# Chunk 1 of x loaded plainly and turned by TensorE, and the second linear layer's queries of chunk 0 computed inside attention 1

## The chip, the cores and the metric

The kernel runs on one core of one Trainium2 chip. The metric is the device time of one execution in microseconds (us), from runs without the profiler; the kernel before takes 2224.86 us (median of three runs, 2223.25 to 2225.45). A core has TensorE (PE, which loads weights beside its matmuls: PEld), VectorE (DVE), ScalarE (ACT), GpSimd (POOL) and SyncE (SP), each with an instruction stream of its own that it works through in order. Transfers are issued from the queues of SP, ACT and POOL and carried by 16 DMA engines.

## The reference

Two layer kinds alternate, A, B, A, B, each added to x (2048 tokens, 1024 features, bf16; 32 heads of 32). The second A and B use the same weights as the first.

```python
def _A_ref(x, wqkv, w_phi, wo):          # linear attention
    q, k, v = qkv[0], qkv[1], qkv[2]     # x @ wqkv, split into heads
    pq = jnp.einsum("bhsd,hdf->bhsf", q, w_phi)
    pk = jnp.einsum("bhsd,hdf->bhsf", k, w_phi)
    phi_q = jnp.concatenate([_softmax(pq, axis=-1), _softmax(-pq, axis=-1)], axis=-1)
    phi_k = jnp.concatenate([_softmax(pk, axis=-1), _softmax(-pk, axis=-1)], axis=-1)
    kv = jnp.einsum("bhsf,bhsd->bhfd", phi_k, v)
    z  = jnp.einsum("bhsf->bhf", phi_k)
    num = jnp.einsum("bhqf,bhfd->bhqd", phi_q, kv)
    den = jnp.einsum("bhqf,bhf->bhq", phi_q, z)[..., None] + 1e-6
    return (num / den) ... @ wo
def _B_ref(x, wqkv, wo):                 # softmax attention
    scores = jnp.einsum("bhqd,bhkd->bhqk", q, k) * (Dh ** -0.5)
    o = jnp.einsum("bhqk,bhkd->bhqd", _softmax(scores, axis=-1), v)
    return o ... @ wo
x = x + _A_ref(_layernorm(x), ...)
x = x + _B_ref(_layernorm(x), ...)
x = x + _A_ref(_layernorm(x), ...)
x = x + _B_ref(_layernorm(x), ...)
```

## The kernel before

x is held in SBUF as xT, features on the partitions, in four chunks of 512 tokens. The four layers run one behind the other as linear stage 1, attention 1, linear stage 2, attention 2, and each pair overlaps at its seam. The weight w_phi is folded into the key and query weights once, in linear stage 1 (fold_phi); the folded weights go to two tensors in HBM, wd_k and wd_q, and are read back as slabs.

Nothing in the code gives the order of the instructions directly. Every operation is recorded with an engine, an estimated duration, its dependencies, its buffers and a priority; then a planner (Sched) plays the engines through and emits each engine's stream in the order in which its model starts them. The tables of numbers at the head of the file are priorities, quotas of buffers and due times for it, so a change to them moves instructions in the whole program. Where the planner finds PE idle in an attention, it inserts filler matmuls: one kind reads xT and onesD (line 616, shared with the layer norms' means), the other xT and zero (line 1788). A unit of PE work is four matmuls of 32 output rows side by side, each 512 columns wide, with the line of mm (L616).

Start. load_x brings chunk 0 of x half by transposing loads on SP (L653) and half by plain loads on POOL that PE turns against the identity (L665); chunks 1, and 2 with 3, come by transposing loads on SP. fold_phi brings the key weight wnat as two quarters on ACT's queue (L825) and one half on POOL's (L828), PE turns it in eight groups (L841), ACT and DVE copy each group out of PSUM (L849, L846), PE folds phi in (L616, reading phi_t), and ACT and DVE copy the folded slab out (L875, L878); SP stores it (L884). The value weights come as slabs on SP (L798). The layer norm of a chunk squares x (L722, L727), sums on PE (L689), and normalizes on DVE (L770, L773 or L778, L782). a_keys then makes a chunk's keys and values for each token tile, their exponentials (L984), the sums (L988) and the products (L945), and kv_sum the state (L911).

Attention 1. A step is up to three score matmuls (L1468), one exponential on ACT that reads them (L1484, 1536 or 1024 wide) and later the products with the values and ones (L1516). Some halves of a step are taken off ACT: exp_dve computes a pair of them by a polynomial on DVE (L1366 twice, then L1375, L1378, L1380, L1383, L1385); COUNT says how many in each turn. Between the steps PE gets the rest as filling work through one PSUM bank, number 7: the keys, values and queries of later turns, the output products of finished chunks, and linear stage 2's layer norms, keys and values of chunks 0, 1 and 2. Results leave bank 7 over DVE (L1216 among others). The normalized chunks 0, 1 and 2 are written to xd in HBM (L1776) and read back in linear stage 2 (L1655).

Linear stage 2. Attention 1's last outputs, the layer norm, keys and values of chunk 3, and the rest of chunk 2's (L1021 to L1036); then for each chunk in two halves the queries: four groups of eight units against wd_q, two exponentials for each group (L1108), their totals (L1119), two logarithms (L1125, L1127), a difference (L1129), its exponential (L1132), a spread over the heads (L1088), the products (L1136, L1151, L1159, L1166, L1171, L1174, L1177); then a_out and the layer norm before attention 2.

## Time and profile before

| | |
|---|---|
| median of 3 runs | 2224.86 us |
| profiled execution | 2226.66 us, span 2224.9 us |
| PE, DVE, ACT, POOL busy in the span | 2153.5, 1803.5, 1968.9, 204.4 us |
| granted TensorE clock | 1.00 of full speed throughout |
| matmuls | 37014 |
| DMA | 111.08 MB, mean 50 GB/s |

A row of the groups reads: line, engine, operation, output<-input, shape and count | busy us, mean ns of one | idle time of the engine before them and who ended it. A row of the windows reads: from:to, length, then for each engine its busy us and, in brackets, its instructions, then the granted clock, the mean busy share of the DMA engines and GB/s. A row of the timeline reads: start, length, engine, line, operation. Busy time of a group is not its count times its mean where matmuls overlap.

### The profile page before, as it was taken

To read this page: it belongs to the slowest core of one execution; us is meant where nothing else is said; L and a number is where in the kernel's file an instruction comes from. 1 tells how busy PE (TensorE), PEld (TensorE's weight loads), DVE (VectorE), ACT (ScalarE), POOL (GpSimd) and SP (SyncE) were. 2 spreads that over 40 slices of the span, in tenths; PEclk is the share of its full clock that TensorE was granted. 3 is DMA by queue.
4 is the path that set the end of the run, shared out by engine and by line. 5 is a ranking of instruction groups with operands and counts; after the bars stand their busy time and mean duration, and the time that the engine had idled before them with its cause. 6 is when DMAs were issued, how large, how long until landed. Compare 5 with 4: busy or idle time off the path is not lost. (4 is left out here: it accounts for less than half of the span.)

```text
span 2224.9 us, 83188 instructions
## 1 busy us (share of the span) xinstructions
PE 2153.5 (97%) x37014; PEld 864.4 (39%) x37014; DVE 1803.5 (81%) x2839; ACT 1968.9 (88%) x1913; POOL 204.4 (9%) x303
## 2 busy tenths in 40 slices
PE   6999999999999999999999999999999999999999
PEld 4554454344333333333333544434333433223333
DVE  6886553597898988785586864599999999999998
ACT  3536668999999999999998667899999999999998
POOL 1010010000002011201224200000000000100000
PEclk9999999999999999999999999999999999999999
DMA  9320111110113122212335101110010011200101
GB/s 201 73 59 10 29 32 32 45 26 19 38 48 109 42 69 73 75 44 73 102 97 154 42 5 32 31 34 22 24 43 21 19 26 29 58 24 28 45 26 38
DMA packets 122256, 111.08 MB, mean 50 GB/s; under 512 B 57960, under 2 KB 107944, under 8 KB 121896
## 3 DMA queue, kind: packets, MB, share of 16 engines
q0 software_dynamic: 17744, 57.23, 9.2%
q1 hardware_dynamic: 101496, 46.96, 8.9%
q8 instruction: 289, 4.73, 0.9%
q10 hardware_dynamic: 2656, 1.57, 0.3%
q14 instruction: 71, 0.58, 0.1%
HBM read 71.11 MB, written 13.89 MB: 38 GB/s over the span
## 5 line engine op out<-in xcount | busy, mean ns | idle before, releaser
L1484 ACT ACTIVATE arena<-psum 128x1536 bf16<-128x1536 f32 (+1 forms) x1339 | 1615.5, 1379 | 21.2 <-PE psum L1516 7.3
L616 PE MATMUL psum<-arena 128*32 128x512 bf16 (+2 forms) x18944 | 1068.9, 352 | 13.0 <-DMA arena<-in_B_wo_dram 3.7
L616 PEld LDWEIGHTS <-arena 128*32 128x32 bf16 x19456 | 462.5, 96 | 441.7 <-issue 177.6
L1516 PE MATMUL psum<-arena 128*32 128x512 bf16 x4096 | 618.8, 383 | 6.2 <-DVE arena L1532 5.9
L1516 PE MATMUL psum<-arena,ones_bf 128*32 128x512 bf16 x4096 | 619.0, 383 | 0.0
L1468 PE MATMUL psum<-arena 32*128 32x512 bf16 x4016 | 528.4, 384 | 18.9 <-ACT arena L1484 14.1
L1468 PEld LDWEIGHTS <-arena 32*128 32x128 bf16 x4016 | 149.0, 91 | 530.7 <-issue 523.7
L1366 DVE TENSOR_SCALAR arena<-psum 128x512 int32<-128x512 f32 x462 | 311.4, 681 | 51.8 <-PE psum L1468 45.8
L1385 DVE SCALAR_TENSOR_TENSOR arena<-arena 128x1024 int16<-128x1024 int32 x231 | 280.2, 1214 | 2.9 <-DVE arena L1383 0.2
L1516 PEld LDWEIGHTS <-arena 128*32 128x32 bf16 x4096 | 164.1, 95 | 219.5 <-issue 166.6
L1516 PEld LDWEIGHTS <-ones_bf 128*32 128x32 bf16 x4096 | 160.8, 95 | 26.3 <-issue 13.0
L1378 DVE TENSOR_TENSOR arena<-arena 128x1024 f16<-128x1024 f16 x231 | 156.6, 681 | 3.1 <-PE psum L616 0.2
L1375 DVE TENSOR_SCALAR arena<-arena 128x1024 f16<-128x1024 int16 x231 | 156.8, 683 | 2.1
L1383 DVE TENSOR_TENSOR arena<-arena 128x1024 f16<-128x1024 f16 x231 | 156.9, 681 | 1.9
L792 POOL DMA_DIRECT2D arena<-in_B_wqkv_dram x46 | 43.3, 944 | 1106.4 <-PE psum L1468 355.6
L1216 DVE CAST arena<-psum 128x512 bf16<-128x512 f32 x132 | 89.9, 681 | 62.0 <-PE psum L616 61.8
L984 ACT ACTIVATE arena<-psum 128x512 bf16<-128x512 f32 x80 | 43.4, 595 | 89.6 <-PE psum L616 72.1
L1380 DVE TENSOR_SCALAR arena<-arena 128x1024 f16<-128x1024 f16 x231 | 96.5, 420 | 1.3
L1532 DVE CAST arena<-psum 128x512 bf16<-128x512 f32 x124 | 84.5, 682 | 9.4 <-PE psum L1516 9.4
L945 DVE TENSOR_TENSOR arena<-psum,arena 128x1024 bf16<-128x1024 f32 x56 | 68.3, 1224 | 21.9 <-PE psum L616 14.7
L1108 ACT ACTIVATE arena<-psum 128x512 bf16<-128x512 f32 x128 | 69.6, 620 | 15.7 <-PE psum L616 15.5
L616 PE MATMUL psum<-xT,onesD 128*32 128x512 bf16 x920 | 80.7, 381 | 1.5 <-DVE xT L1294 0.6
(134 smaller groups left out, 1298.8 us busy)
## 6 DMA issues: line engine op xcount, KB each, us to landing
arena<-in_B_wqkv_dram POOLq DMA_DIRECT2D x58, 256.0 KB, 4.2
arena<-in_B_wo_dram POOLq DMA_DIRECT2D x40, 256.0 KB, 4.2
arena<-in_A_wqkv_dram POOLq DMA_DIRECT2D x36, 256.0 KB, 4.2
arena<-arena SPq DMA_DIRECT2D x256, 32.0 KB
arena<-wd_k POOLq DMA_DIRECT2D x32, 256.0 KB, 4.6
arena<-rd SPq DMA_DIRECT2D x62, 128.0 KB
arena<-arena SPq DMA_DIRECT2D x96, 64.0 KB
arena<-arena SPq DMA_DIRECT2D x248, 1.0 KB
```

The costliest lines, as they stand in the source:

```text
L616: nc.tensor.matmul(out_[ks, :], lhsT=lhsT[:, ks], rhs=rhs, start=start, stop=stop, tile_position=(0, 32 * k), skip_group_check=True)
L1216: return op("DVE", dve_us(512), lambda: nc.vector.tensor_copy(out=dst(), in_=src()), [dep], bufs, prio)
L1366: o = op("DVE", dve_us(512), lambda: nc.vector.tensor_scalar(out=x_v()[:, k, :].bitcast(I32), in0=s_v()[:, x * C512:(x + 1) * C512], scala ...
L1375: last = op("DVE", 1024 / 1920 + 0.15, lambda: nc.vector.tensor_scalar(out=z(), in0=x_v().bitcast(I16).rearrange("p a (n two) -> p a n two ...
L1378: last = op("DVE", 1024 / 1920 + 0.15, lambda: nc.vector.tensor_tensor(out=u(), in0=z(), in1=z(), op=ALU.mult), [last], [z_b, u_b], prio + ...
L1380: last = op("DVE", 1024 / 3840 + 0.15, lambda: nc.vector.tensor_scalar(out=u(), in0=u(), scalar1=POW2_C[0], scalar2=POW2_C[1], op0=ALU.mul ...
L1383: last = op("DVE", 1024 / 1920 + 0.15, lambda: nc.vector.tensor_tensor(out=u(), in0=z(), in1=u(), op=ALU.mult), [last], [z_b, u_b], prio + ...
L1385: return op("DVE", dve_us(1024), lambda: nc.vector.scalar_tensor_tensor(out=y_v().bitcast(I16), in0=x_v().bitcast(I32), scalar=128.0 / BIT ...
L1468: nc.tensor.matmul(out=s_v()[:, x * C512:(x + 1) * C512], lhsT=kT[g][1]()[r, pp, d * P:(d + 1) * P], rhs=q_of[(qc, g)][1]()[r, (pp + j // ...
L1484: ex = op("ACT", act_us(w * C512), lambda s_v=s_v, e_v=e_v, w=w: nc.scalar.activation(out=e_v(), in_=s_v()[:, 0:w * C512], func=ACT.Exp, s ...
L1516: nc.tensor.matmul(out=a_v()[col:col + 32, :], lhsT=v_v()[:, kc % 4, o:o + DH] if what == 0 else ones_bf[:], rhs=ev()[:, x * C512:(x + 1) ...
L1532: cp = op("DVE", dve_us(512), lambda t_v=t_v, a_v=a_v: nc.vector.tensor_copy(out=t_v(), in_=a_v()), [last], [a_b, t_b], prio - 4)
```

## The change

1. load_x loads chunk 1 with four plain loads of 128 tokens on POOL's queue (xnat), PE turns them in 32 transposes and ACT copies them out (four copies). The transposing loads of chunks 2 and 3 depend on those four loads.
2. fold_phi loads the key weight's first half as one transfer on ACT's queue, and its second half on SP's instead of POOL's; the second half's four groups are all copied out by ACT.
3. A new function a_soon computes chunk 0's queries of linear stage 2 in attention 1, group by group through bank 7 and DVE, and writes them to xd in place of the normalized chunk. In linear stage 2, a_queries of chunk 0 (ready) takes its 16 exponentials from what was read back, without matmuls.
4. b_o's second part waits for its first part's sum. Nearly every number of the planner's tables is another one: priorities, quotas, the seed of its ties, COUNT (94 to 97 in the sum for attention 1, 143 to 141 for attention 2).

```diff
-TIE = 3
+TIE = 8
...
-PULL = (3.1, 2.1)
-PULLN = 16
+PULL = (5.7, 19.9)
+PULLN = 15
+QSOON = (0,)
+QAT = ((221.2, 1.1, 0.4), (263.3, -16.6, 16.8), (285.6, -4.2, -0.9))
+X1 = ('GQ', -4.0, 1.0)
...
+        n1b, n1v = sb("xnat", TB, D)
+        nat1 = [dma(-16.0, lambda t=t: ENG[X1[0]].dma_start(
+            out=n1v()[:, t, :], in_=A_x[0, C512 + t * P:C512 + (t + 1) * P, :]), (), [n1b], q=X1[0], kb=256, issue=0.75)
+            for t in range(TB)]
...
+            for pr in range(4 if lo == 1 else 0):
+                tb, tv = ps("wt", ANY)
...
+                t1 = None
+                for t in range(TB):
+                    t1 = op("PE", 2 * 0.11, lambda t=t, tr1=tr1: tr1(t), [nat1[t], t1], [tb, n1b], X1[1] + X1[2] * pr, mode="n", ni=4)
+                last += [op("ACT", act_us(1024) + 0.06, lambda pr=pr, tv=tv: nc.scalar.copy(
+                    out=xT[:, 2 * pr:2 * pr + 2, C512:2 * C512],
...
-            for po in range(PO if lo else PO // 2):
+            for po in range(0 if lo == 1 else PO if lo else PO // 2):
                 last.append(dma(
...
-                    issue=us, kb=kb))
+                    deps=nat1 if lo else (), issue=us, kb=kb))
...
+            ld.append([dma(-24.0, lambda: nc.scalar.dma_start(out=nv()[:, :, 0:C512], in_=A_w[:, :, col:col + C512]),
+                           (), [nb], q="AQ", kb=1024, issue=0.7)])
...
+            ld.append([dma(-20.0, lambda i=i: nc.sync.dma_start(
...
+            if ready:
+                k = 4 * hf + a
+                ex = [op("ACT", act_us(512) + 0.1, lambda s=s, k=k, ev=ev: nc.scalar.activation(
+                    out=ev()[:, s, :], in_=xv()[:, k, :], func=ACT.Exp, scale=(1.0, -1.0)[s]),
+                    [fin[k // 2]], [xb, eb], pre) for s in range(2)]
+                eq.append((eb, ev, ex))
+                continue
...
+    def a_soon(c, prio, x, gaps):
+        xb, xv, fin = x
+        away = []
+        for k in range(G):
+            pr = prio + gaps[1] * k + gaps[2] * (k // 4)
+            if k % 4 == 0:
+                wb, ww, wd = slab("slabk", pr - 1.0, wdq_v[:, :, k // 4 * C512:(k // 4 + 1) * C512], C512, [store["q"][k // 4]])
+            pb, pv = ps("fil", FIL)
+            m = mmg2(pb, pv, lambda po, k=k, ww=ww: ww()[:, po, k % 4 * P:k % 4 * P + P], lambda po: xv()[:, po, :], fin, wd, [xb, wb], pr)
+            a_b, a_v = sb("kt", C512)
+            cp = evac("DVE", a_v, pv, m, [pb, a_b], pr)
+            d = dma(pr, lambda k=k, a_v=a_v: nc.gpsimd.dma_start(out=xd_v[:, c, k, :], in_=a_v()), [cp], [a_b], q="GQ", kb=128)
+            d.slack = 3.0
+            away.append(d)
+        return [away[2 * i:2 * i + 2] for i in range(4)]
...
-                 [[oT[2 * i][2], oT[2 * i + 1][2], after] for i in range(4)], wd,
+                 [[oT[2 * i][2], oT[2 * i + 1][2], after, part[2] if part else None] for i in range(4)], wd,
...
-                a_queries(c, hf, pr + 5 * hf, wq_s, state, oc, (EARLY[layer], *EARLYC[layer])[c])
+                a_queries(c, hf, pr + 5 * hf, wq_s, state, oc, (EARLY[layer], *EARLYC[layer])[c], layer and c in QSOON)
...
+                if c in QSOON:
+                    xnA[c] = a_soon(c, at + QAT[c][0], (xb, xv, fin), QAT[c])
+                    continue
```

What stands where on the engines, at the three places that the prediction speaks of. The first is SP's stream from the program's start, before (xT is x turned, wd_k the folded key weights):

```order
L653 DMA_TRANSPOSE xT<-in_A_x_dram 128x512 x10
L798 DMA arena<-in_A_wqkv_dram 128x2x512 x8
L884 DMA wd_k<-arena 128x2x512
L653 DMA_TRANSPOSE xT<-in_A_x_dram 128x512 x2
L653 DMA_TRANSPOSE xT<-in_A_x_dram 128x1024
```

and after (L673 is L653 before, L818 is L798, L902 is L884; L846 is the key weight's second half):

```order
L673 DMA_TRANSPOSE xT<-in_A_x_dram 128x512 x4
L846 DMA arena<-in_A_wqkv_dram 128x2x512 x4
L673 DMA_TRANSPOSE xT<-in_A_x_dram 128x1024 x3
L818 DMA arena<-in_A_wqkv_dram 128x2x512 x8
L902 DMA wd_k<-arena 128x2x512
```

Of the first ten transposing loads the six of chunk 1 are gone, four plain loads of the key weight have come in, and three loads of chunks 2 and 3 now stand ahead of the value weights.

The second is POOL's stream in attention 1, after (L818 loads slabs, L968 is a small copy of linear stage 2's keys, L1217 stores a group of queries):

```order
L818 DMA arena<-wd_q 128x2x512 x2
L968 CAST arena<-arena 128x32 x2
L818 DMA arena<-wd_q 128x2x512 x5
L1217 DMA xd<-arena 128x512
L968 CAST arena<-arena 128x32 x2
L818 DMA arena<-wd_q 128x2x512
L1217 DMA xd<-arena 128x512
L1792 DMA arena<-in_B_wo_dram 128x2x1024
L1217 DMA xd<-arena 128x512 x3
L818 DMA arena<-wd_k 128x2x512 x2
```

Before, no load from wd_q and no store of queries stands in this stretch; the eight rows of wd_q and eight stores of 128x512 are new, and four stores of chunk 0 (128x1024) are gone.

The third is ACT's stream at the beginning of linear stage 2, before:

```order
L727 ACTIVATE arena<-xT 128x1024 x4
L753 ACTIVATE arena<-psum 128x512
L755 CAST arena<-psum 128x512
L758 ACTIVATE arena<-arena,eps 128x512
L760 ACTIVATE arena<-arena 128x512
L984 ACTIVATE arena<-psum 128x512 x2
L1021 ACTIVATE arena<-arena 128x2x512 x2
```

and after (L747 is L727 before, L773 is L753, L775 is L755, L778 is L758, L780 is L760, L1039 is L1021; L1125 is an exponential of chunk 0's queries as read back):

```order
L747 ACTIVATE arena<-xT 128x1024 x3
L1125 ACTIVATE arena<-arena 128x512 x2
L747 ACTIVATE arena<-xT 128x1024
L773 ACTIVATE arena<-psum 128x512
L775 CAST arena<-psum 128x512
L1125 ACTIVATE arena<-arena 128x512 x2
L1039 ACTIVATE arena<-arena 128x2x512 x2
L1125 ACTIVATE arena<-arena 128x512
L778 ACTIVATE arena<-arena,eps 128x512
L1125 ACTIVATE arena<-arena 128x512
L780 ACTIVATE arena<-arena 128x512
L1125 ACTIVATE arena<-arena 128x512 x3
```

The 16 exponentials of chunk 0 now stand among the last chunk's layer norm and ahead of most of its keys' exponentials. Behind the last chunk's keys (the last L911), PE's stream has 1840 matmuls of L616 512 columns wide before the first score of attention 2, where it had 2072; ahead of them, from attention 1's end, it has 768 in both. Over the whole program PE has 160 filler matmuls fewer (L616 on xT and onesD 920 to 828, L1788 428 to 360), that is 40 units, and 32 transposes more. On ACT six exponentials 1536 wide became 1024 wide in attention 1, and two the other way in attention 2.

110 lines of the change are left out of this document (54 added, 56 removed).

## The prediction

> **What bounds the kernel now.** I read the page's totals first, then a table of the stages, then what releases TensorE at the start, then the groups by form.
>
> ```profile
> span 2224.9 us, 83188 instructions
> PE 2153.5 (97%) x37014; PEld 864.4 (39%) x37014; DVE 1803.5 (81%) x2839; ACT 1968.9 (88%) x1913; POOL 204.4 (9%) x303
> ```
>
> 97% for PE is an average over stages with different limits, and part of it is filler. The view of busy time in windows, cut where the limit changes:
>
> ```profile
> core 0: us, PE busy (x) PEld busy (x) DVE busy (x) ACT busy (x) POOL busy (x), PEclk, DMA share, GB/s
> 0.00:20.00 20.00, 3.53 (x28) 2.74 (x28) 7.05 (x32) 2.29 (x2) 7.45 (x16) 1.00 1.02 176
> 20.00:38.00 18.00, 13.65 (x371) 9.79 (x375) 13.12 (x21) 13.16 (x21) 0.00 (x0) 1.00 1.15 227
> 38.00:340.00 302.00, 297.92 (x6624) 156.08 (x6617) 205.78 (x291) 169.52 (x283) 29.02 (x58) 1.00 0.23 52
> ...
> 420.00:720.00 300.00, 296.88 (x4740) 112.25 (x4737) 256.61 (x412) 298.14 (x248) 20.55 (x24) 1.00 0.18 48
> 720.00:1080.00 360.00, 348.47 (x5257) 119.62 (x5256) 284.44 (x430) 356.56 (x296) 54.43 (x75) 1.00 0.23 64
> ...
> 1208.00:1258.00 50.00, 48.39 (x1272) 27.75 (x1268) 49.69 (x60) 24.10 (x38) 22.11 (x38) 1.00 0.35 109
> 1258.00:1410.00 152.00, 150.46 (x2902) 68.84 (x2898) 87.34 (x142) 109.41 (x176) 4.68 (x6) 1.00 0.06 16
> ...
> 1440.00:2190.00 750.00, 735.50 (x11307) 262.28 (x11299) 740.10 (x1210) 744.35 (x638) 22.80 (x26) 1.00 0.12 31
> ```
>
> To 38 us the DMA engines are full (share 1.02 to 1.15) and PE starves: 17.2 of 38 us busy. From 38 to 340 us (linear stage 1) PE is the limit, 98.6% busy. In attention 1 ACT is (99% in both rows), with PE 11.5 us and DVE 75.6 us idle between 720 and 1080. In 1208:1258 (the last chunk's keys of linear stage 2) DVE is, 49.69 of 50; in 1258:1410 (its queries, outputs and layer norms) PE is, 150.46 of 152, while ACT has 42.6 us idle. In attention 2 ACT and DVE are both near 99%. So an edit pays in each stage by what it takes from that stage's limit.
>
> **The start.** Rows of the timeline (start, length, engine) and one of PE's waits before 38 us:
>
> ```profile
> 0.75 20.27 SPq L653 DMA_TRANSPOSE xT<-in_A_x_dram  x10
> 0.77 5.25 ACTq L825 DMA_DIRECT2D arena<-in_A_wqkv_dram  x2
> 5.35 1.44 POOL L828 DMA_DIRECT2D arena<-in_A_wqkv_dram  x2
> 20.55 1.89 PE L841 MATMUL psum<-ident,arena 128*128 128x128 bf16 x16 [8.77 <-DMA arena<-in_A_wqkv_dram]
> 21.07 4.57 SPq L798 DMA_DIRECT2D arena<-in_A_wqkv_dram  x8
> 37.34 5.37 PE L616 MATMUL psum<-arena 128*32 128x512 bf16 x96
> 42.75 3.65 PE L616 MATMUL psum<-arena 128*32 128x512 bf16 x64
> 46.21 0.40 PE L911 MATMUL psum<-arena 128*32 128x33 bf16 x32
> ...
> PE psum L841 <- DMA arena<-in_A_wqkv_dram: 14.2, 2, 8.8
> ```
>
> The weight's second quarter, issued on ACT's queue by 6.0 us, releases PE only at 20.55: it shares the engines with ten transposing loads on SP. At 37.34 the first token tile's keys and both folds of phi are done and PE runs on without gaps. The two rows at 42.75 and 46.21 give the unit: 64 matmuls in 3.46 us, 0.216 us for four that run side by side.
>
> The change takes the eight transposing loads of chunk 1 off SP (1 MB), adds four plain loads of 256 KB on POOL, 32 PE transposes and four ACT copies; the weight's first half is one load with rows of 1 KB instead of two with 512 B, and its second half moves from POOL to SP, behind chunk 0's four transposing loads. Costs from these rows, the first two being PE's groups before 38 us and the rest windows:
>
> ```profile
> L841 PE MATMUL psum<-ident,arena 128*128 128x128 bf16 x64 | 6.2, 266 | 15.6 <-DMA arena<-in_A_wqkv_dram 14.2 <-issue 0.9 <-ACT arena L755 0.4
> L616 PE MATMUL psum<-phi_t,arena 128*32 128x128 bf16 x256 | 5.5, 220 | 2.2 <-issue 1.5 <-ACT arena L849 0.3 <-DVE arena L846 0.3
> ...
> 6.00:14.00 8.00, 2.96 (x25) 2.16 (x22) 1.98 (x3) 1.01 (x1) 2.24 (x4) 1.00 1.01 130
> 14.00:18.00 4.00, 0.00 (x0) 0.00 (x0) 1.29 (x2) 0.00 (x0) 0.00 (x0) 1.00 1.07 287
> 24.00:30.00 6.00, 5.09 (x166) 3.78 (x159) 3.96 (x7) 5.49 (x11) 0.00 (x0) 1.00 1.02 320
> ...
> 40.00:54.00 14.00, 14.00 (x376) 8.37 (x372) 10.45 (x12) 4.57 (x9) 1.31 (x4) 1.00 1.20 198
> ```
>
> Before the equivalent point (first tile's keys, both folds, chunk 1 turned) the new order needs 4 MB: weight 2, chunk 0 and chunk 1 one each. At the 176 GB/s of 0:20 (3.5 MB in 20 us) they are in at 22.7 us; at the 287 of 14:18 after 6 us at 176 (1 MB) at 16.5; at the 130 of 6:14 for the last 3 MB at 29. Behind them PE has 32 weight transposes (16 took 1.89, so 3.8), a tile of keys (8 units, 1.7), a fold (half of 5.5, 2.8) and the 32 new transposes (3.8): 12.1 us. The point comes at 28.6, 34.8 or 41.1 against 37.34: a gain of 8.7 or 2.5, or a loss of 3.8. I take 4.5: the four slow loads that held the 130 GB/s stretch are fewer, and the weight's last blocks need not be last of the 4 MB. SP now waits there for POOL's four loads, and queued behind that wait are three transposing loads (20.27 us for ten, so 6 us), then the value weights (L798, issued at 21.07 before), then wd_k's stores. With POOL's loads in at 16.5 to 22.7 us, L798 is issued from 22.6 to 28.8, and the first half (1 MB at 198 to 320 GB/s) is in at 26 to 34; values are first needed just after the point, at 29 to 35. So the wait just hides; a longer one is in the lower bound.
>
> In the Trainium skill, Advanced Engine Details and Errata, section X-Bar Transpose (TRN2), transposing loads are said to be as fast as regular ones; by that no DMA time comes free here. The row 40:54, where little but transposing loads runs, shows 198 GB/s at a share of 1.20, against 320 at 1.02 for 24:30, where plain loads prevail, so the trace does not bear it out.
>
> **Queries in attention 1.** 64 units move (8 groups of 8, each with 4 matmuls): 64 x 0.216 = 13.8 us of PE. Further rows by form, with fillers of 720:1080 last:
>
> ```profile
> L1484 ACT ACTIVATE arena<-psum 128x1536 bf16<-128x1536 f32 x876 | 1216.4, 1526 | 16.0 <-PE psum L1468 5.6 <-PE psum L1516 4.7 <-DMA arena<-arena 3.7
> L1484 ACT ACTIVATE arena<-psum 128x1024 bf16<-128x1024 f32 x463 | 470.6, 1103 | 5.2 <-PE psum L1516 2.7 <-PE psum L1468 0.8
> L616 PE MATMUL psum<-arena 128*32 128x512 bf16 x14336 | 919.6, 381 | 11.3 <-DMA arena<-in_B_wo_dram 3.7 <-DVE arena L1216 2.0 <-DVE arena L1310 1.0
> L1366 DVE TENSOR_SCALAR arena<-psum 128x512 int32<-128x512 f32 x462 | 311.4, 681 | 51.8 <-PE psum L1468 45.8 <-ACT arena L1484 4.6 <-issue 1.0
> ...
> L1385 DVE SCALAR_TENSOR_TENSOR arena<-arena 128x1024 int16<-128x1024 int32 x231 | 280.2, 1214 | 2.9 <-DVE arena L1383 0.2 <-ACT arena L1484 0.2
> L1383 DVE TENSOR_TENSOR arena<-arena 128x1024 f16<-128x1024 f16 x231 | 156.9, 681 | 1.9
> L1216 DVE CAST arena<-psum 128x512 bf16<-128x512 f32 x132 | 89.9, 681 | 62.0 <-PE psum L616 61.8
> ...
> L616 PE MATMUL psum<-xT,onesD 128*32 128x512 bf16 x224 | 20.3, 380 | 0.0
> L1788 PE MATMUL psum<-xT,zero 128*32 128x512 bf16 x180 | 14.6, 379 | 0.0
> ```
>
> The room: of the 224 matmuls with onesD 64 belong to layer norms (32 for a chunk, two chunks there), so 160 + 180 are filler, 85 units or 18.4 us, beside 11.5 us of idle PE. The order after has 40 filler units fewer in the whole program, nearly all of them here, 8.7 us; the other 5.1 us must come out of the idle time. Eight evacuations (8 x 0.681 = 5.4 us) and three pairs of exponentials moved from ACT to DVE (each 2 x 0.681 + 1.214 + four steps no longer than L1383's 0.681, so up to 5.3; 15.9 for three) lie in DVE's 75.6 us idle. The eight loads of wd_q and eight 128 KB stores instead of four of 256 KB go on POOL, 54.43 us busy of 360.
>
> ACT gains: six of its 1536-wide instructions become 1024-wide. Busy time over count gives 1.389 and 1.016 us, so 6 x 0.373 = 2.2 us. With cover gone (PE late for ACT) the 5.1 us are paid instead. I take a gain of 1.5 between 2.2 and a loss of 5.1, near the former since ACT's own waits in the two L1484 rows sum to 21 us over the whole run. If an evacuation is late, PE stands with the next scores behind it; L616's waits on L1216 sum to 2.0 us for 132.
>
> **Linear stage 2.** In 1208:1258 the limit is DVE's work, which stays but for one instruction more of the 0.68 us class. PE keeps its 768 matmuls of L616 there, fed by chunk 1's queries in place of chunk 0's, and gets about 0.7 us of small ones; I charge 0.9. Sixteen exponentials come forward onto ACT:
>
> ```profile
> L1132 ACT ACTIVATE arena<-arena 128x512 bf16<-128x512 f32 x8 | 5.0, 629 | 4.5 <-DVE arena L1129 4.4
> ```
>
> 16 x 0.63 = 10 us lie in ACT's 25.9 idle us of that row. They wait for the queries read back from xd, and the layer norm's squares and the keys' exponentials stand behind them. Behind the keys, in the PE-bound stage, the order has 1840 such matmuls instead of 2072: 58 units, 12.5 us; small moves net out to nothing. The lost matmuls were also cover for the chain of each query half, exponential to logarithm to spread to product; three halves now follow each other closer, and I charge 1.5 us for PE waiting (bounds: 0, and 6 for all the chain's slack). 12.5 - 0.9 - 1.5 = 10.1, say 10, between 5 and 12.5.
>
> **Attention 2** gets two 1536-wide for two 1024-wide, 0.75 us on ACT, and one pair less on DVE; its first steps stand a microsecond or two earlier on PE. I charge 0.5, between -1.5 and 1. The new numbers also reorder instructions everywhere else; their counts are the same, and the wait that b_o's second half gains is for a partial sum formed long before it. I give this nothing, and 2 us either way in the range.
>
> **Sum**: -4.5 - 1.5 - 10 + 0.5 = -15.5 us. The profiled execution took 2226.66 us for its span of 2224.9 (1.8 around it) and would take 2211.2; the median of the runs, 2224.86, lies 1.8 below it, so 2209.4.
>
> **The rivals.** (a) The start gives nothing: loads of both kinds cost the engines the same, the 4 MB come no sooner, and the 3.8 us of transposes are paid. For it: the DMA share is already 1.0 from 2 us on; against: 198 against 320 GB/s. -15.5 + 4.5 + 3.8 = -7.2, so 2217.7. This is what the time would be by the Trainium skill's rule named above.
> (b) In linear stage 2 the chain through ACT and DVE replaces PE as the limit: chunk 0's and 1's halves then pace at ACT's and DVE's work and only 3 of 10 us come through: -8.5, 2216.4. For it: ACT is 72% busy there; against: it loses work in that stage too. (a) and (b) together give -0.2, no change.
> (c) Slower: query groups in attention 1 share bank 7 and DVE's in-order queue. If half of the eight evacuations stand behind a whole pair (5.0 us), PE and then ACT stop for 20 us: -15.5 + 20 = +4.5, 2229.4. It decides from 1.9 us lost in each of the eight upward. Against it: 2.0 us in 132 evacuations so far.
>
> **How the numbers follow.** Forecast 0.60, (a) 0.13, (b) 0.15, both 0.06, (c) 0.06. The range 2201 to 2219: the start's best (8.7) and linear stage 2's best (12.5) give 2202.7 and attention 2's bound 2200.7; above it takes in (a) and (b). About 0.2% (4.5 us) is what a measurement tells from no change. Faster: forecast, (a) and (b), less 0.02 for their tails, 0.86; same 0.08; slower 0.06.
>
> **What would show it.** At the start: PE gap-free from about 33 us instead of 37, and L841's wait on its weights far below 14.2 us. In attention 1: fillers down by about 40 units, ACT idle no larger than before. From the end of the last chunk's keys to the first step of attention 2: about 11 us shorter with PE still near 99%. Wrong would be: value weights that PE waits for at 30 us, L1216's evacuations as releasers of PE in attention 1, or ACT waiting for arena<-xd at 1210.

## The result, and the profile after

The changed kernel takes 2212.86 us (median of 4 runs, 2210.16 to 2213.96); the kernel before, run beside it on the same chip, 2224.06 (2222.75 to 2225.45). The ratio is 0.9947, 95% interval 0.9934 to 0.9960, some 12 us faster. The profiled execution has a span of 2212.0 us against 2224.9, 12.9 shorter. Six points of the two traces split it: the first exponential of attention 1, the end of attention 1 (where ACT first starts a copy of 64x256, L1551, now L1592), the last state product (L911, now L929), the first wide exponential of attention 2 (L1484, now L1525), the start of the last exponential, the end.

| us | before | after | difference | predicted |
|---|---|---|---|---|
| start to attention 1's first exponential | 345.2 | 341.2 | -4.0 | -4.5 |
| attention 1 | 858.4 | 858.6 | +0.2 | -1.5 |
| last chunk's keys | 55.2 | 56.5 | +1.3 | +0.9 |
| behind the keys, to attention 2 | 160.7 | 151.6 | -9.1 | -11 |
| attention 2's exponentials | 793.5 | 791.4 | -2.1 | +0.5 |
| after the last exponential | 11.9 | 12.7 | +0.8 | 0 |

The page's totals after, and windows cut at these points, first of before, then of after (the columns are those of the prediction's windows):

```profile
span 2212.0 us, 82973 instructions
PE 2149.6 (97%) x36886; PEld 855.4 (39%) x36886; DVE 1818.5 (82%) x2859; ACT 1971.4 (89%) x1919; POOL 207.0 (9%) x315
```

```profile
345.00:1203.00 858.00, 838.78 (x13060) 303.72 (x13061) 660.77 (x1025) 848.38 (x696) 115.17 (x155) 1.00 0.22 62
...
1258.80:1419.50 160.70, 158.81 (x3227) 74.28 (x3211) 92.22 (x150) 117.06 (x186) 5.72 (x8) 1.00 0.07 17
```

```profile
341.00:1199.00 858.00, 843.31 (x13134) 303.31 (x13129) 678.38 (x1053) 845.44 (x695) 118.54 (x164) 1.00 0.23 65
...
1256.30:1407.90 151.60, 148.81 (x3000) 67.91 (x2983) 90.63 (x149) 107.17 (x168) 5.52 (x7) 1.00 0.08 19
```

Behind the keys PE is still the limit, 148.8 of 151.6 us. It works 10.0 us less and stands 2.8 us instead of 1.9. In attention 1 ACT works 2.9 us less (848.38 to 845.44) in the same 858 us, so it stands 2.9 us more.

**The start after**, PE's and SP's rows of the timeline up to the point that the prediction named (x96; before it stood at 37.34), and five windows:

```profile
9.35 0.61 PE L685 MATMUL psum<-ident,arena 128*128 128x128 bf16 x4 [9.35 <-DMA arena<-in_A_x_dram]
11.92 1.46 PE L685 MATMUL psum<-ident,arena 128*128 128x128 bf16 x12 [1.96 <-DMA arena<-in_A_x_dram]
...
26.27 0.61 PE L859 MATMUL psum<-ident,arena 128*128 128x128 bf16 x8 [0.79 <-ACT arena L867]
27.18 1.91 PE L618 MATMUL psum<-arena 128*32 128x512 bf16 x32 [0.31 <-ACT arena L867]
...
35.49 5.47 PE L618 MATMUL psum<-arena 128*32 128x512 bf16 x96 [0.31 <-ACT xT L668]
```

```profile
6.24 4.25 SPq L846 DMA_DIRECT2D arena<-in_A_wqkv_dram  x4
11.98 9.20 SPq L673 DMA_TRANSPOSE xT<-in_A_x_dram  x3
21.23 4.99 SPq L818 DMA_DIRECT2D arena<-in_A_wqkv_dram  x8
```

```profile
0.00:6.00 6.00, 0.00 (x0) 0.00 (x0) 3.77 (x27) 1.28 (x1) 5.22 (x14) 1.00 0.74 202
6.00:12.00 6.00, 0.69 (x6) 0.43 (x6) 0.00 (x0) 0.00 (x0) 1.00 (x2) 1.00 1.14 150
12.00:18.00 6.00, 5.79 (x44) 3.14 (x44) 3.94 (x7) 1.01 (x1) 0.54 (x1) 1.00 1.09 278
18.00:24.00 6.00, 4.37 (x150) 3.26 (x149) 4.99 (x9) 5.38 (x10) 0.00 (x0) 1.00 1.22 224
24.00:30.00 6.00, 4.90 (x128) 3.74 (x127) 3.77 (x7) 5.82 (x9) 0.00 (x0) 1.00 1.00 308
```

The wait of L841 (now L859) on its weights, 14.2 us before, is gone: PE works from 12 us on with gaps of 1.1 us at most, and from 32.24 on with one gap of 0.31. The point comes at 35.49, 1.85 us sooner than before. From 18 to 30 us ACT is busy 11.2 of 12 us, and three of the small waits name its copies (L867, L668). The value weights (L818) go out at 21.23, as before at 21.07.

**Attention 1**: ACT's two main waits for PE before, and after; then PE's filler groups before, and after (busy us, mean ns | idle before them):

```profile
ACT arena L1484 <- PE psum L1516: 4.9, 6, 2.9
ACT arena L1484 <- PE psum L1468: 2.7, 7, 0.7
```

```profile
ACT arena L1525 <- PE psum L1509: 7.1, 12, 2.1
ACT arena L1525 <- PE psum L1557: 2.8, 3, 1.7
```

```profile
L616 PE MATMUL psum<-xT,onesD 128*32 128x512 bf16 x280 | 24.8, 380 | 0.6 <-DVE arena L945 0.5
L1788 PE MATMUL psum<-xT,zero 128*32 128x512 bf16 x216 | 17.9, 379 | 0.0
```

```profile
L618 PE MATMUL psum<-xT,onesD 128*32 128x512 bf16 x200 | 16.4, 381 | 0.6 <-DVE arena L963 0.6
L1830 PE MATMUL psum<-xT,zero 128*32 128x512 bf16 x140 | 11.9, 380 | 0.0
```

Fillers fell by 156 matmuls, 39 units. PE's idle time in the 858 us fell from 19.2 to 14.7. ACT waits more often for scores (L1468, now L1509), 7.1 us instead of 2.7.

**The keys, and attention 2's beginning.** Rows of PE's timeline in the keys after; behind them ACT's rows at the beginning of attention 2 before, and after:

```profile
1215.15 2.77 PE L618 MATMUL psum<-arena 128*32 128x512 bf16 x48 [1.29 <-DMA arena<-xd]
1219.03 1.91 PE L618 MATMUL psum<-arena 128*32 128x512 bf16 x32 [1.11 <-DMA arena<-xd]
```

```profile
1419.54 2.80 ACT L1484 ACTIVATE arena<-psum 128x1536 bf16<-128x1536 f32 x2
1426.09 11.34 ACT L1484 ACTIVATE arena<-psum 128x1536 bf16<-128x1536 f32 x9 [3.74 <-DMA arena<-arena]
```

```profile
1407.92 23.98 ACT L1525 ACTIVATE arena<-psum 128x1536 bf16<-128x1536 f32 x20 [0.60 <-PE psum L1509]
```

Chunk 1's normalized x is now the first that PE needs from xd, and PE waits 2.4 us for it; before, no row in this stretch waits for xd. In attention 2 the stop of 3.74 us behind the first exponentials is gone.

### The profile page after: what moved, and what is told of

It is laid out like the page before. It is cut to its first block, busy times and chain, and to the rows that moved or that the text cites. A ratio compares the mean times of both kernels' runs of the same rounds, so it can differ in the third digit from the quotient of the medians.

```text
span 2212.0 us, 82973 instructions
## 1 busy us (share of the span) xinstructions
PE 2149.6 (97%) x36886; PEld 855.4 (39%) x36886; DVE 1818.5 (82%) x2859; ACT 1971.4 (89%) x1919; POOL 207.0 (9%) x315
## 5 line engine op out<-in xcount | busy, mean ns | idle before, releaser
L1525 ACT ACTIVATE arena<-psum 128x1536 bf16<-128x1536 f32 (+1 forms) x1339 | 1613.0, 1386 | 22.5 <-PE psum L1509 12.9
L1557 PE MATMUL psum<-arena 128*32 128x512 bf16 x4096 | 621.2, 383 | 6.3 <-DVE arena L1573 5.1
L1557 PE MATMUL psum<-arena,ones_bf 128*32 128x512 bf16 x4096 | 621.3, 383 | 0.0
L1509 PE MATMUL psum<-arena 32*128 32x512 bf16 x4016 | 528.2, 384 | 16.4 <-ACT arena L1525 12.8
L1509 PEld LDWEIGHTS <-arena 32*128 32x128 bf16 x4016 | 147.3, 91 | 530.3 <-issue 522.3
L1557 PEld LDWEIGHTS <-arena 128*32 128x32 bf16 x4096 | 164.3, 95 | 216.5 <-issue 166.3
L1557 PEld LDWEIGHTS <-ones_bf 128*32 128x32 bf16 x4096 | 160.6, 95 | 31.3 <-issue 12.7
L1257 DVE CAST arena<-psum 128x512 bf16<-128x512 f32 x140 | 95.4, 682 | 52.5 <-PE psum L618 52.3
L1002 ACT ACTIVATE arena<-psum 128x512 bf16<-128x512 f32 x80 | 43.6, 597 | 81.0 <-PE psum L618 65.1
L1573 DVE CAST arena<-psum 128x512 bf16<-128x512 f32 x124 | 84.6, 682 | 14.2 <-PE psum L1557 13.8
L1133 ACT ACTIVATE arena<-psum 128x512 bf16<-128x512 f32 x112 | 61.1, 625 | 16.1 <-PE psum L618 15.4
L1231 DVE TENSOR_TENSOR xT<-xT,psum 128x512 bf16<-128x512 bf16 x64 | 42.9, 684 | 38.8 <-PE psum L618 36.3
```

What stands on the lines that cost most here:

```text
L1257: return op("DVE", dve_us(512), lambda: nc.vector.tensor_copy(out=dst(), in_=src()), [dep], bufs, prio)
L1509: nc.tensor.matmul(out=s_v()[:, x * C512:(x + 1) * C512], lhsT=kT[g][1]()[r, pp, d * P:(d + 1) * P], rhs=q_of[(qc, g)][1]()[r, (pp + j // ...
L1525: ex = op("ACT", act_us(w * C512), lambda s_v=s_v, e_v=e_v, w=w: nc.scalar.activation(out=e_v(), in_=s_v()[:, 0:w * C512], func=ACT.Exp, s ...
L1557: nc.tensor.matmul(out=a_v()[col:col + 32, :], lhsT=v_v()[:, kc % 4, o:o + DH] if what == 0 else ones_bf[:], rhs=ev()[:, x * C512:(x + 1) ...
L1573: cp = op("DVE", dve_us(512), lambda t_v=t_v, a_v=a_v: nc.vector.tensor_copy(out=t_v(), in_=a_v()), [last], [a_b, t_b], prio - 4)
```

## The experiments

Each run's ratio is to the kernel before, run beside it, with its 95% interval. Spans and stages are of the one profiled execution. Since a change to code or numbers lets the planner draw the whole order anew, there are two kinds: those in which the order was kept and one thing in it was changed (p1 to p4), and those with a new order (the others). One execution's start is not exact to 2 us: p1 has after's start in after's order and reaches attention 1 at 339.2, after at 341.2. Stages in us, in the order of the table above:

| run | ratio | start | attention 1 | keys | behind | attention 2 | end |
|---|---|---|---|---|---|---|---|
| before | 1 | 345.2 | 858.4 | 55.2 | 160.7 | 793.5 | 11.9 |
| after | 0.9947 | 341.2 | 858.6 | 56.5 | 151.6 | 791.4 | 12.7 |
| p1, p4 (after's order) | 0.9960, 0.9943 | 339.2, 340.4 | 860.2, 857.6 | 59.6, 56.4 | 152.6, 151.6 | 791.3, 791.8 | 12.6, 12.7 |
| p2, p3 (before's order) | 0.9996, 0.9992 | 344.7, 343.7 | 856.7, 857.2 | 56.2, 55.4 | 160.6, 160.5 | 791.9, 793.8 | 11.9, 12.0 |
| e1 | 0.9976 | 340.3 | 864.0 | 55.3 | 151.5 | 789.9 | 14.2 |
| e2 | 0.9967 | 339.0 | 855.3 | 54.4 | 163.0 | 792.5 | 12.6 |
| e6, s1 (after, other seeds) | 0.9973, 0.9982 | 339.9, 339.9 | 864.2, 862.1 | 55.6, 59.6 | 151.9, 150.9 | 791.4, 793.9 | 12.9, 13.5 |
| e7, s2 (before, other seeds) | 0.9994, 1.0045 | 342.3, 340.7 | 860.0, 864.2 | 54.8, 55.5 | 159.8, 159.7 | 792.4, 797.5 | 12.5, 13.5 |
| e8 | 1.0018 | 338.9 | 868.4 | 63.4 | 152.9 | 789.8 | 13.1 |
| e5 | 1.0017 | 339.8 | 869.2 | 57.4 | 152.4 | 796.8 | 12.8 |

### One part undone

`e1_old_start`: the changed kernel with the old load_x, the old weight loads in fold_phi and their two tables (WK, WT).

```diff
-WK = (0.0, 1.5)
+WK = (0.8, 2.0, 3.5)
+WT = (-28.2, -28.0, -11.3, -15.3)
...
-            for po in range(0 if lo == 1 else PO if lo else PO // 2):
+            for po in range(PO if lo else PO // 2):
```

> The changed kernel with load_x and fold_phi as before (chunk 1 by transposing loads, the key weight's quarters on ACT's and POOL's queues); everything else as changed. Theory: the new start is worth what the two traces show between 0 and the first step of attention 1 (345.2 to 341.2 us), so 4 us come back: 2217, first score exponential of attention 1 at about 345. Rival (a), transposing loads cost the engines nothing extra and the 32 PE transposes are paid: undoing the start gains, 2209 to 2212. Rival, the new tables of numbers made the gain and not the start: 2213 within 1.5.

Measured: 2219.89 us, 0.9976 (0.9966 to 0.9985). The first exponential of attention 1 comes at 340.3, no later than with the new start (341.2, and 338.9 to 340.4 in the other runs that have it). What was lost against after is in attention 1 (864.0 against 858.6), where this code does nothing: the total came within 3 us of the theory's 2217, but not by the theory's way.

`e2_no_soon`: the changed kernel without chunk 0's queries in attention 1.

```diff
-QSOON = (0,)
+QSOON = ()
```

> The changed kernel with QSOON empty: chunk 0's queries are made in linear stage 2 again, the start and all numbers stay as changed. Theory: moving 64 units out of the PE-bound stage gave 8 to 10 us, so 2221 to 2223, with the time from the last state sum of linear stage 2 to the first step of attention 2 back near 160 us from 151.6. Rival: the numbers (PULL above all, by which attention 2's first steps come earlier) gave that stage its shorter time and the queries little: 2213 to 2216.

Measured: 2218.0 us, 0.9967 (0.9957 to 0.9978). The stretch behind the keys is back at 163.0 us, 161.60 of it PE's work (after: 148.81 of 151.6):

```profile
1248.70:1411.70 163.00, 161.60 (x3248) 73.02 (x3232) 92.36 (x150) 118.08 (x189) 4.64 (x6) 1.00 0.07 18
```

That is 11.4 us more than after and 11.1 to 12.1 more than e1, e6 and s1. Attention 1 is the shortest of all, 855.3, and the keys 54.4. So the queries bring some 11 us where they were and cost something where they went; the total, 4.5 us below after's gain, is less than the 11.

`e6_seed`: the changed kernel with before's seed of the planner's ties, as a gauge for what a new order alone does.

```diff
-TIE = 8
+TIE = 3
```

> The changed kernel with only the planner's tie seed set back (TIE 8 to 3). Theory: another seed moves instructions everywhere but no work, so the time stays within 2 us of 2212.9. Rival: the particular seed is worth several us, and part of the measured gain is its luck: 2216 or more.

Measured: 2218.16 us, 0.9973 (0.9964 to 0.9983): 5.8 us of the gain are gone with no work changed, 5.6 of it in attention 1. So the totals of e1 and e2, each a new draw, don't measure the parts; their stages do where they agree over all draws.

`e8_dve_copies`: chunk 1's four copies out of PSUM on DVE, so planned.

```diff
-                last += [op("ACT", act_us(1024) + 0.06, lambda pr=pr, tv=tv: nc.scalar.copy(
+                last += [op("DVE", 0.69, lambda pr=pr, tv=tv: nc.vector.tensor_copy(
```

> The changed kernel with the four copies of chunk 1 out of PSUM on DVE instead of ACT. Theory: the start gained 1.9 us instead of 4.5 because ACT took the place of the loads as limit (it is full from 20 to 52 us, with 3.8 us of these copies and 3.8 us of weight copies in it); then the first long run of keys and values on PE starts at about 33.5 us instead of 35.5 and the time falls to 2211. Rival: PE's own order and its data set the point: it stays at 35.5 and the time at 2213; or DVE, busy 1.6 to 2 of each 2 us from 32 to 50, becomes the limit: 2213 to 2215.

Measured: 2228.66 us, 1.0018 (1.0008 to 1.0027). The start is early (338.9), and 9.8 us are lost in attention 1 and 6.9 in the keys, far from the copies; both theories had put the time at 2215 or less. Whether the copies or the new order did it, p4 tells.

### One thing changed in a kept order

`p1_soon_light`: the changed kernel's order, but of each of the eight query groups' eight units only the last is issued; chunk 0's queries are not what they should be.

```diff
+                    if light:
+                        if po == 7:
+                            mm(pv(), lhs(po), rhs(po), True, True, cols)
+                        continue
```

> The changed kernel with its instructions in the same order, but each of the eight groups of a_soon issues one unit of its eight (56 units, 12.1 us of PE, left out; chunk 0's queries of linear stage 2 are then not the reference's). Evacuations, stores and loads stay. Theory: in attention 1 the queries displace filler and idle time but not all of it, and 2 to 4 us of them are paid there (attention 1 took 858.6 us from its first step to its end though ACT has 2.2 us less to do); without them 855 to 857 and 2209 to 2211 in all. Rival: they are wholly hidden: 858.6, 2213. Rival (c) and a PE-bound attention 1: 847 to 850, 2201 to 2205.

Measured: 2216.4 us, 0.9960 (0.9945 to 0.9975). 56 units, 12.1 us of PE, are taken out of attention 1, and the kernel is not faster than after (0.9947). In this order the added matmuls are hidden. One thing blurs it: TensorE's granted clock falls to half in p1's trace from 932 to 938 us, where ACT has 3.9 of the 10 us from 930 idle, and all four executions have a mean granted clock of 0.997 or 0.998, where after's and p4's have 0.999. By the relation in the last section that is an estimated 3 us, so a gain of that size could be covered, but not 12.

`p2_queries_light`: before's order, with one of eight units of chunk 0's queries of linear stage 2 issued (the same `light` in the stage of a_queries); those queries are not what they should be either.

```diff
-                     fin, qd, [xb, qb], pre)
+                     fin, qd, [xb, qb], pre, light=layer == 1 and c == 0)
```

> The kernel before with its instructions in the same order, but chunk 0's queries of linear stage 2 issue one unit of eight (56 units, 12.1 us of PE, left out; these queries are then not the reference's). Theory: PE bounds the stage behind the last chunk's keys, but about half of chunk 0's queries lie ahead of them where DVE is the limit; so 5 to 7 us come off in all, 2217 to 2220. Rival: all of PE's time there is the limit: 11 to 12 us, 2212 to 2214. Rival (b), the chain through ACT and DVE: 0 to 4 us, 2220 to 2224.

Measured: 2224.1 us, 0.9996 (0.9986 to 1.0006). Taking 12.1 us of PE's work out of before gains nothing that is clear of noise. (The mean granted clock of its executions is 0.9975 against 0.9989 for before beside it, an estimated 2 us by the relation in the last section; so a few us may be covered, but not 12.) Two windows of p2, behind the keys and in them:

```profile
1257.60:1418.20 160.60, 157.00 (x3156) 72.75 (x3144) 92.37 (x150) 116.75 (x185) 6.43 (x8) 1.00 0.07 17
1201.40:1257.60 56.20, 46.98 (x1199) 24.98 (x1203) 53.25 (x64) 29.08 (x48) 23.44 (x40) 0.94 0.35 107
```

and PE's groups of 512-wide matmuls in the keys, of before and of p2:

```profile
L616 PE MATMUL psum<-arena 128*32 128x512 bf16 x768 | 45.5, 380 | 1.7 <-DVE arena L1310 0.8 <-DMA arena<-in_B_wo_dram 0.6 <-DVE xT L1294 0.2
```

```profile
L616 PE MATMUL psum<-arena 128*32 128x512 bf16 x620 | 40.2, 400 | 1.8 <-DVE arena L1314 0.8 <-DMA arena<-in_B_wo_dram 0.4 <-ACT arena L984 0.3
```

148 of the 224 matmuls taken out stood in the keys, where DVE is the limit (53.25 of 56.2) and PE now only idles. The other 76 (4.1 us) stood behind them; PE does 1.8 us less there and the stretch is no shorter; the 1.8 us became idle time in its first 16 us, where PE now waits for steps of the query chain on ACT and DVE (1.7 us of named waits). So the gain of after does not come from the queries being out of linear stage 2 alone, but from chunk 1's queries, which move up into the free PE time of the keys and so leave the PE-bound stretch. PE's group in the keys after is as large as before's:

```profile
L618 PE MATMUL psum<-arena 128*32 128x512 bf16 x766 | 45.5, 380 | 3.1 <-DMA arena<-xd 2.4 <-DVE arena L1596 0.5 <-DVE xT L1335 0.2
```

`p3_plain_same`: before's order, with chunk 1's eight transposing loads replaced by plain loads of the same bytes on the same queue; chunk 1 then lies in xT in a wrong layout.

```diff
-                    prio, fn=lambda lo=lo, hi=hi, po=po: nc.sync.dma_start_transpose(
+                    prio, fn=lambda lo=lo, hi=hi, po=po: nc.sync.dma_start(
+                        out=xT[:, po, C512:2 * C512], in_=A_x[0, C512 + (po // 2) * P:C512 + (po // 2 + 1) * P, po % 2 * C512:(po % 2 + 1) * C512]) if lo == 1 else nc.sync.dma_start_transpose(
```

> The kernel before with its instructions in the same order, but the eight transposing loads of chunk 1 are plain loads of the same bytes from the same tokens on the same queue (chunk 1 is then laid out wrongly and the output is not the reference's). Theory: transposing loads hold the DMA engines longer for their bytes (198 against 320 GB/s); the weight's second quarter then releases PE's second group of transposes at 15 to 18 us instead of 20.55, the first long run of keys and values comes 2 to 4 us earlier than 37.34, and the time falls to 2220 to 2222. Rival (a): they are as fast as plain loads: 20.5, 37.3 and 2224 to 2225.

Measured: 2224.27 us, 0.9992 (0.9983 to 1.0002), no change. Its trace says why. SP's rows, two windows and a row of PE of p2, whose loads are those of before, and the same of p3:

```profile
0.75 19.46 SPq L653 DMA_TRANSPOSE xT<-in_A_x_dram  x10
20.25 4.17 SPq L798 DMA_DIRECT2D arena<-in_A_wqkv_dram  x8
...
12.00:18.00 6.00, 0.00 (x0) 0.00 (x0) 1.29 (x2) 0.00 (x0) 0.00 (x0) 1.00 1.15 266
18.00:24.00 6.00, 4.18 (x60) 3.18 (x64) 1.98 (x3) 1.01 (x1) 0.00 (x0) 1.00 1.00 207
...
19.82 1.89 PE L841 MATMUL psum<-ident,arena 128*128 128x128 bf16 x16 [8.81 <-DMA arena<-in_A_wqkv_dram]
```

```profile
5.95 6.86 SPq L653 DMA_DIRECT2D xT<-in_A_x_dram  x6
12.85 8.18 SPq L799 DMA_DIRECT2D arena<-in_A_wqkv_dram  x8
...
12.00:18.00 6.00, 0.00 (x0) 0.00 (x0) 1.29 (x2) 0.00 (x0) 0.00 (x0) 1.00 1.08 325
18.00:24.00 6.00, 4.85 (x84) 3.85 (x88) 2.21 (x4) 1.60 (x2) 0.00 (x0) 1.00 1.10 347
...
19.15 1.89 PE L842 MATMUL psum<-ident,arena 128*128 128x128 bf16 x16 [7.96 <-DMA arena<-in_A_wqkv_dram]
```

Plain loads are the cheaper ones: 325 and 347 GB/s where the transposing loads leave 266 and 207, at shares of 1.00 to 1.15, and six leave SP's queue in 6.86 us where ten transposing ones took 19.46. By the packets of the two traces, 256 bytes of a transposing load keep a DMA engine 31 to 38 ns and 1 KB of a plain load from SP 51 to 54. The room seems to have gone to the transfers next in the queue: the value weights go out at 12.85 instead of 20.25 us, beside the weight's second quarter that PE waits for, whose transposes (L841, in p3 L842) start at 19.15 against 19.82. That is 0.7 us, no more than lies between p2 and before, whose loads are the same (19.82 and 20.55). No run held the value weights back, so that they took the room is read from the order of the queue and not shown.

`p4_dve_copies_kept`: after's order, with the four copies of chunk 1 on DVE.

```diff
-                last += [op("ACT", act_us(1024) + 0.06, lambda pr=pr, tv=tv: nc.scalar.copy(
+                last += [op("ACT", act_us(1024) + 0.06, lambda pr=pr, tv=tv: nc.vector.tensor_copy(
```

> The changed kernel in the same order, with the four copies of chunk 1 issued on DVE at their places instead of ACT. Theory: ACT, full from 20 to 52 us, set the start's gain, and PE's transposes of chunk 1 wait for nothing else; the first long run of keys and values comes at 33 to 35 us instead of 35.5 and the time falls by 0.5 to 2 us to 2211 to 2212.5. Rival: DVE, which the order did not plan for them, delays the first products: 2213 to 2216. The 15 us that the kernel with newly planned DVE copies lost would then not come from the copies but from its other order: both theories give far less than 15.

Measured: 2211.95 us, 0.9943 (0.9928 to 0.9958), as after. At the start its one trace lies 0.8 us ahead of after's (340.4 against 341.2), less than the 2.0 us between after and p1, so a gain there can't be read; the total shows none. And e8's 16 us in the total belong to its order, not to the copies.

### The seed and the tables

Three more draws: before with the seeds 8 and 1, after with the seed 1 (`e7_seed_before`, `s2_before_tie1`, `s1_after_tie1`).

```diff
-TIE = 3
+TIE = 8
```

> The kernel before with the planner's seed of ties at 8 in place of 3, all else kept. If the tables of numbers are fitted to one drawn order: 3 to 8 us slower than before, 2228 to 2233 us. If the seed is worth nothing and the 6 us that the changed kernel lost with another seed belong to its new parts: within 2.5 us of before, 2222.5 to 2227.5.

Measured: 2223.93 us, 0.9994 (0.9984 to 1.0003).

```diff
-TIE = 3
+TIE = 1
```

> The kernel before with the seed at 1, a third draw of the same tables. Fitted tables: 3 to 8 us slower than before, 2228 to 2233. Seed worth nothing: 2222.5 to 2227.5. Should the two other seeds fall on both sides of before, the seed is a draw of some us and not a fit.

Measured: 2235.2 us, 1.0045 (1.0030 to 1.0060), 5.8 us lost in attention 1 and 4 in attention 2.

```diff
-TIE = 8
+TIE = 1
```

> The changed kernel with the seed at 1 in place of 8. Fitted tables: as with seed 3, some 5 us slower than with 8, 2215 to 2220. Seed 3 an unlucky one: 2211 to 2215. In both cases the stretch from the last chunk's keys to attention 2's first exponential stays at 151 to 153 us, since the 58 units left it in any order; the loss then lies in attention 1 and the keys.

Measured: 2221.38 us, 0.9982 (0.9973 to 0.9991).

Neither theory holds for before as it was put: one other seed costs nothing, the next 10 us. After's own seed is its best of three, by 6 and 8 us. So a seed is a draw of some us, with a good one in the tables as they stand. The mean of the three ratios is 1.0013 for before ((1 + 0.9994 + 1.0045) / 3) and 0.9967 for after ((0.9947 + 0.9973 + 0.9982) / 3), 0.0046 or 10 us apart. The mean stages of the same six traces differ by -2.4 (start), +0.8 (attention 1), +2.1 (keys), -8.6 (behind), -2.2 (attention 2) and +0.4 us. Of these only the stretch behind the keys is clear of the scatter (159.7 to 160.7 in before's three draws, 150.9 to 151.9 in after's). The keys are longer after, if barely (54.8 to 55.5, 55.6 to 59.6); the start overlaps (340.7 to 345.2, 339.9 to 341.2), and so do the others. With three draws on each side the 10 us are themselves uncertain by several us.

`e5_old_numbers`: the edits of the code with the tables of before; only the three new ones (QSOON, QAT, X1) and the shorter WK were added.

```diff
+QSOON = (0,)
+QAT = ((221.2, 1.1, 0.4), (263.3, -16.6, 16.8), (285.6, -4.2, -0.9))
+X1 = ('GQ', -4.0, 1.0)
```

> All edits of the code with the tables of before (COUNT, PULL and the rest, seed 3), and only the three new tables of the change added. If the edits carry the gain and the other numbers only fit the order: the stretch behind the keys is 150 to 154 us against 160.7, and the time is 2212 to 2222. If the gain needs the new numbers as a whole: 2222 or more, with the queries of chunk 0 or their stores late somewhere in attention 1.

Measured: 2229.4 us, 1.0017 (1.0007 to 1.0026). The stretch behind the keys has its gain (152.4) and the start too (339.8), and attention 1 loses 10.8 us against before. ACT's groups there:

```profile
L1525 ACT ACTIVATE arena<-psum 128x1536 bf16<-128x1536 f32 x488 | 672.7, 1518 | 14.7 <-PE psum L1557 7.8 <-PE psum L1509 5.6 <-DVE arena L1426 0.8
L1525 ACT ACTIVATE arena<-psum 128x1024 bf16<-128x1024 f32 x184 | 187.9, 1097 | 3.1 <-PE psum L1557 1.3 <-DVE arena L1424 0.6 <-PE psum L1509 0.4
```

ACT stands 17.8 us before them (14.7 + 3.1), mostly for products and scores that come late from PE; in the same two groups of after it is 12.6 (8.9 + 3.7). By the windows of whole stages ACT works 851.4 us of e5's 869.2 and 846.2 of after's 858.6: of the 10.6 us between them 5.2 are work and 5.4 waiting. So a good part of what the new numbers do, it seems, is to place the added work where PE has time. What part of that is COUNT's and what part the priorities' was not tried.

## Why the prediction was right, point by point

The total came out inside the range: 2212.86 against 2209.4, -11.2 us by the runs made side by side and -12.9 by the spans, where -15.5 was forecast. The sign and the place of the gain were right, and four of five terms were somewhat off.

**The start** (-4.5 forecast, -1.85 at the named point, -4.0 at the first exponential). The step that failed is the 12.1 us of PE behind the 4 MB, taken as if nothing but PE paced them. In after's trace the last load of chunk 1 lands at 18.84 us, sooner than the 22.7 of the middle case, and PE waits for no load from there on. To the point it takes 16.65 us more, 12.1 of them PE's work, as much as was charged, and 4.6 idle. The sum had nothing for idle time; of it 2.1 end with ACT, 1.0 with DVE and 1.1 with nothing that the profile names. For most of the time (18 to 30 us) ACT is 93% busy, with the copies of the weight and the folds and with the layer norm. p4 shows no gain from taking the four copies of chunk 1 off ACT; whether the other copies are it was not tried. Rival (a) is half right. The difference that the prediction read (198 against 320 GB/s) is real: p3's plain loads move more (325 against 266), so the rule of the Trainium skill (Advanced Engine Details and Errata, X-Bar Transpose (TRN2)) that both kinds are equally fast is not borne out. (The prediction's row 40:54 is no pure case: 1.1 of its 2.7 MB are stores of the folded key weights.) But p3's time is unchanged all the same, it seems because the room goes to the next loads in the queue. That the value weights' wait is hidden was right: no row of PE waits for them at 30 us. Between the point and the first exponential 2.1 us more were gained, which the prediction had not. And -4.0 against a forecast of -4.5 is in part luck: it sets the latest of all traces with the old start against the latest with the new. With the old start attention 1 begins at 340.3 to 345.2 (before, p2, e7, s2, e1; mean 342.6), with the new one at 338.9 to 341.2 (eight traces, mean 339.8), some 3 us apart. The one trace with the old start and the new tables, e1, lies at 340.3, among the new ones, so what part of the 3 us is the loads' and what part the order's is open.

**Attention 1** (-1.5 forecast, +0.2). Each part of the step is in the trace: 39 units of filler fewer (40 forecast), 4.5 us out of PE's idle time (5.1), ACT's work 2.9 us less (2.2). The size that failed is the wait: ACT stands 2.9 us longer, mainly for scores (2.7 to 7.1), which eats the gain. It is no loss through the queries' matmuls themselves, as far as p1 tells. The evacuations of rival (c) are no releasers here: PE's waits for them (L1216, now L1257) sum to 1.6 us over the run against 2.6 before. Its price does exist, by another way: in e5 the products and scores themselves come late, and attention 1 is 10.8 us longer.

**Linear stage 2** (-11 behind the keys and +0.9 in them, measured -9.1 and +1.3). 58 units fewer are there (2072 matmuls 512 wide before, 1840 after), and 0.9 us more of waiting, against the 1.5 charged for the chain. The term that was too large is the 12.5, taken as if nothing else came in: PE's work falls by 10.0, and 16 products of attention 2 (L1516, now L1557, 2.0 us by their two groups), of which this stretch had none before, stand here now. Rival (b) fell: PE is 98% busy. In the keys it is DVE, the limit there, that has more to do: 54.9 us in 66 instructions, where it had 53.2 in 64; the prediction had one instruction of 0.68 us more. The new wait in the keys is for xd, as was feared, but on PE (2.4 us, chunk 1's read-back) and not on ACT.

**Attention 2** (+0.5 forecast, -2.1). The stop of 3.74 us in the row 1426.09 of before, for a transfer from one buffer in SBUF to another, was not costed: it is gone after. In the three draws of each the difference is -2.2 with a scatter of 5, so whether it stays so is open.

**The reordering** was given nothing, and 2 us either way. That is the step with the largest error: draws of one and the same work spread over 0.0051 of the time, 11 us, for before and 0.0035, 8 us, for after. With seed 8 the new tables have the best of three draws, so that the total came so near is in part luck. Over three draws each, edits and new tables together are worth about 10 us. Neither does it alone in the draws at hand: the edits with the old tables (e5) are 4 us slower than before, and the new tables without the queries (e2, with the new start) 7 us faster. The new tables with none of the edits were not tried.

## What to carry to other kernels

Taking work off a busy engine pays only where that engine is the limit, or if the order refills what it leaves: p2 took 12 us out, most of it where DVE was the limit, and gained nothing clear of noise, while the change put chunk 1's queries where chunk 0's had covered a DVE-bound stretch, and gained 9 behind it. Where a planner places every instruction, gauge it with two or three seeds on each side before judging a part by its total; undo a part in the kept order, or read the stage and not the total. And in p3 cheaper loads brought the awaited one no sooner than scatter: what stands next in the queue starts in their place, so look at it before counting freed DMA time as a gain.

## What the runs showed of the hardware

The granted clock of TensorE drops to half for some microseconds in the middle of a busy stage, at times after idle times of little more than 1 us. A row of after's timeline of PE in attention 2, and the windows from there on:

```profile
2012.45 0.38 PE L1557 MATMUL psum<-arena 128*32 128x512 bf16 x1 [1.09 <-DVE arena L1573]
```

```profile
2012.00:2014.00 2.00, 1.55 (x18) 0.41 (x17) 2.00 (x4) 1.96 (x3) 0.00 (x0) 0.96 0.05 9
2014.00:2016.00 2.00, 2.00 (x22) 0.40 (x23) 1.85 (x4) 1.94 (x3) 0.00 (x0) 0.50 0.20 66
2016.00:2018.00 2.00, 2.00 (x27) 0.66 (x23) 1.08 (x3) 0.77 (x1) 0.00 (x0) 0.69 0.00 0
```

ACT, the limit there, loses 1.23 us of the last window. e2, p1, p4 and s1 have such a stretch within 10 us of the same place, e5, e7 and s2 one near 1084, and p1, s1, e1 and e8 one between 1201 and 1211, after 2.2 to 3.2 us idle at the end of attention 1; before, p3 and e6 have none until the program's end. By the traces' records of the clock each is 3.41 or 6.83 us long, and those of one trace lie a whole number of 3.41 us apart. In the 3.41 us ahead of each (18 in all, those in the last 5 us of a program left out) PE is busy for 22 to 62% (after: 1.93 us of 2010.42 to 2013.83), so all idle time in such a step fits better than the longest gap. But as idle a step passes without half clock too (49% busy at 1423.5 in before, 43% at 1208.7 in e5), so what trips it is open.

An execution's time goes with its mean granted clock. Before was run in three groups beside the experiments, 73 times in all; where the mean clock was 1.000 it took 2222.4, 2223.8 and 2223.8 us in the mean of each group, where it was 0.998 it took 2226.2, 2227.0 and 2227.7. Over all kernels with eight executions or more, each about its own mean, the slope is some 1.5 us for 0.001. It isn't what sets the draws apart: e6 lost its 5.6 us in attention 1 without a stretch of half clock, and but for p1 and p2 no run's mean lies more than 0.001 from that of before beside it.

p2 has such a stretch in its keys, behind a longer idle time:

```profile
1217.18 0.43 PE L911 MATMUL psum<-arena 128*32 128x33 bf16 x32 [3.41 <-DVE arena L1031]
```

```profile
1218.00:1220.00 2.00, 2.00 (x24) 0.74 (x20) 2.00 (x4) 0.00 (x0) 0.00 (x0) 0.50 0.96 377
```

There PE had been given less to do, and did the rest more slowly (400 ns for a 512-wide matmul in the group above, 380 in before). The Trainium skill (TensorE: Matmul & The Clock Gate, Part 1) tells of half clock after an idle window of about 3.4 us. p2's idle time is that long, though by the record its half clock begins at 1216.42, 2.65 us after PE's last matmul. The 1.09 us of after, with 0.39 us at 2010.97, are shorter than that.
